# Batch 0's scores with keys on partitions, and no row maximum where a bound allows it

## The chip, the cores and the metric

One core of a Trainium2 chip runs the kernel. Its engines are TensorE (PE, with PEld for its weight loads), VectorE (DVE), ScalarE (ACT), GpSimd (POOL) and SyncE (SP), which only issues DMAs here. The metric is device time in microseconds (us) of one execution.

## The reference

Eight batches, twelve heads, 448 positions, heads of 64. Queries and keys are normalised by their root mean square and multiplied by gains, then softmax attention; its output x (448 x 768 per batch) goes through a channel mix. The weights are float64.

```python
q_n, k_n = (rmsnorm(q, g_q), rmsnorm(k, g_k))          # x / sqrt(mean(x*x) + 1e-06) * g
scores = matmul(q_n, k_n.transpose(0, 1, 3, 2)) / sqrt(64)
scores = scores - max(scores, axis=-1, keepdims=True)
attn = exp(scores)
attn = attn / (sum(attn, axis=-1, keepdims=True) + 1e-09)
x = matmul(attn, v)                                    # heads side by side
x_prev = x one position earlier, zeros first
xk = mu_k * x + (1 - mu_k) * x_prev
xr = mu_r * x + (1 - mu_r) * x_prev
kk = maximum(xk @ w_k, 0.0)                            # w_k: 768 x 1024
vv = kk * kk @ w_v                                     # w_v: 1024 x 768
r = 1 / (1 + exp(-(xr @ w_r)))                         # w_r: 768 x 768
out = r * vv
```

A normalised row of 64 has a norm of at most 8, so a score is at most 8 * 8 / sqrt(64) = 8 times the largest |g_q g_k|, or 64 times the largest |g_q g_k| / 8.

## The kernel before, in words

**A planner sets the order.** Every part of the kernel is a Python generator that yields operations (one, or a list of matmuls). `Plan.run` repeatedly takes the generator whose operation could start soonest by the planner's own clocks, less a bonus for its priority, and `emit` (line 272) issues it right behind the last one on its engine. So every engine executes a list that was fixed when the program was built, an instruction waits for all those ahead of it on its engine, and every row of the trace carries line 272: the parts are told apart by the tile names. Where either of two engines can do an operation, `plan.pick` takes the one with the lower planned clock.

**Units.** A pair is two heads of a batch (48 in all), a quad is two pairs (24, numbered u). Quads 0 to 2 are batch 0 (`U32 = 3`). A quad's scores come in seven groups of two 128 x 448 tiles, one per head; the seventh holds the last 64 query rows of both pairs.

**Attention.** `stats` and `preps` norm q and k; `turn` transposes them on PE through an `sc` bank into tile `stk`. `scores` issues a group with queries on partitions; `expo` takes a row maximum on DVE (`sums<-sc`, negated) and the exponential on ACT with the maximum as bias and the row sum accumulated beside it.

- Batch 0 stays in float32 end to end (one product per score). The exponentials go to a `nat` tile in SBUF; `probs_pe` scales and inverts the sums on DVE (`sums<-sums`), normalises on POOL (`nat<-nat,sums`), transposes 128 x 128 blocks on PE into `sc` banks (`sc<-ident,nat`), and ACT or DVE copies them into `pT` (`pT<-sc`). `attends` then issues 16 float32 products per pair (`ot<-pT,vf`; on PE they stand in runs of eight records) into the only `ot` bank, and ACT copies the result into the pair's tile `x`.
- Batches 1 to 7 use float16 in three terms (high x high, high x low, low x high). The exponentials stay in PSUM (`sc<-sc,sums`); `split` makes the normalised high half on ACT (`nat<-sc,sums`) and the remainder on DVE (`nat<-sc,sums,nat`); SP's DMA queue transposes `nat` into `pT`; 24 products per pair follow.

**Weights.** `weights` turns 20 column tiles (8 of w_k, 6 of w_r, 6 of w_v, each in two halves) from float64 into float32: POOL takes the top three bits of the low word from its byte 3, ACT scales the high word by 2^-112 into an `mm` bank with Prelu (its slope for negative numbers puts the sign where the next step keeps it), and DVE shifts the one by three and joins the other (`wf<-mm,raw`). `wsplit` finds each column's scale (a product of the tile with itself, its diagonal `dg`, a product `mm<-dg,ones` that spreads it, a DVE maximum `WSC`), and splits the tile into two float16 halves (`wvl<-wf,WSC,wvh` and the like).

**Channel mix.** `mix` makes xk and xr (`df<-x,bsc,df` on DVE). `moe` takes one batch after the other: products with w_k (`mm<-xk,wkh`), relu and square, and then products with w_r and w_v. Before batch 0's first product with w_r it waits until all 20 weight tiles are done (`wdone == NW`).

**Buffers.** Five PSUM banks `sc`, two `mm`, one `ot`; in SBUF 2 `raw`, 2 `wf`, 4 `nat`, 4 `stk`, 9 `x`; `pT` has two halves, one per pair of a quad (`PTFREE`). Until `moe` starts, room of xk, kk and others is lent to `raw`, `wf`, `nat`, `vf`, so some tiles read `xk_104` or `kk_108` early in the program.

## Time and profile before

| | |
|---|---|
| median of 3 runs | 1023.7 us (1022.6 to 1023.84) |
| the profiled execution, span | 1022.8 us |
| PE busy | 933.2 us, 91% |
| DVE busy | 789.3 us, 77% |
| ACT busy | 748.2 us, 73% |
| POOL busy | 691.6 us, 68% |
| DVE row maxima of scores | 336 in 194.3 us |
| ACT exponentials in PSUM | 294 in 180.9 us |
| DVE second halves of the split | 242 (of 294, other shapes apart) in 158.3 us |

How to read the rows: `L272 DVE TENSOR_REDUCE sums<-sc 128x1 f32<-128x448 f32 x336 | 194.3, 614 | ...` is line, engine, operation, output <- inputs by tile name, output shape and input shape (partitions x elements), count; behind the first bar busy time in us and mean ns of one; behind the second the idle time of the engine just ahead of them and what ended most of it. In the slices each digit is a fortieth of the span in tenths busy; PEclk is TensorE's granted clock in tenths of full speed.

### The profile page before, as it was taken

The numbers are of one execution on the slowest core, as the hardware profiler recorded it, in microseconds if no ns is written. First come the engines' busy times: TensorE is split into PE (matmuls) and PEld (weight loads), VectorE is DVE, ScalarE is ACT, GpSimd is POOL, SyncE is SP. The second block draws the span as 40 slices with busy tenths as digits, with TensorE's granted clock in tenths as the row PEclk, the third lists the DMA queues.
The fourth block names the chain that finished last, engine by engine and source line by source line (L and its number), as shares of the span: only waits on it lengthen the run. The fifth ranks groups of instructions, "written<-read, shape, count | busy, mean of one in ns | idle before, by whom it ended". The sixth has DMA issues, their size and how long they took to land.

```text
span 1022.8 us, 18968 instructions
## 1 busy us (share of the span) xinstructions
PE 933.2 (91%) x6166; PEld 489.2 (48%) x6166; DVE 789.3 (77%) x1967; ACT 748.2 (73%) x1755; POOL 691.6 (68%) x738
## 2 busy tenths in 40 slices
PE   1678778778999899999999999999999999999997
PEld 1344334344554455445555555455455554455564
DVE  5888868998989689878988798969887898785000
ACT  2666748988789688798888788888887887684211
POOL 2587678862688576896788467967795679629501
PEclk9779889978999999999999999999999999999999
DMA  8442348785885797777986889579768986662011
GB/s 200 121 118 74 104 126 173 181 182 112 188 188 125 150 188 155 171 165 173 185 165 113 179 180 190 127 163 193 157 126 179 183 181 139 135 124 54 1 32 31
DMA packets 447043, 146.62 MB, mean 143 GB/s; under 512 B 418784, under 2 KB 443360, under 8 KB 446944
## 3 DMA queue, kind: packets, MB, share of 16 engines
q1 hardware_dynamic: 427408, 127.42, 59.2%
q10 hardware_dynamic: 19536, 18.00, 6.1%
q8 instruction: 48, 0.79, 0.3%
q14 instruction: 51, 0.42, 0.1%
HBM read 50.40 MB, written 11.01 MB: 60 GB/s over the span
## 4 chain that ended last, share of the span: by engine, by line
PE 54%; DVE 18%; ACT 9%; POOL 7%; issue 6%; DMA 4%; SPq 1%; ACTq 0%; POOLq 0%; DVEq 0%
PE mm L272 37%; PE ot L272 9%; PE sc L272 8%; DVE sums L272 4%; DVE nat L272 3%; POOL xk L272 2%; ACT nat L272 2%; ACT sc L272 2%; DVE sst L272 2%; DVE df L272 2%; DMA pT<-nat 1%; DVE stm L272 1%; POOL nat L272 1%; SPq L272 1%; POOL qk L272 1%
## 5 line engine op out<-in xcount | busy, mean ns | idle before, releaser
L272 PE MATMUL mm<-wvh,kk 128*128 128x384 f16 x896 | 234.4, 327 | 0.0
L272 PE MATMUL mm<-xk,wkh 128*128 128x448 f16 x768 | 209.5, 355 | 5.9 <-ACT kf L272 4.2
L272 DVE TENSOR_REDUCE sums<-sc 128x1 f32<-128x448 f32 x336 | 194.3, 614 | 23.4 <-PE sc L272 23.0
L272 ACT ACTIVATE sc<-sc,sums 128x448 f32<-128x448 f32 x294 | 180.9, 617 | 36.9 <-DVE sums L272 33.1
L272 ACT ACTIVATE nat<-sc,sums 128x448 f16<-128x448 f32 (+1 forms) x274 | 167.2, 653 | 24.9 <-DVE sums L272 13.1
L272 PE MATMUL mm<-wrh,xr 128*128 128x384 f16 x672 | 179.9, 331 | 0.0
L272 DVE SCALAR_TENSOR_TENSOR nat<-sc,sums,nat 128x448 f16<-128x448 f32 x242 | 158.3, 675 | 28.0 <-ACT nat L272 27.5
L272 PEld LDWEIGHTS <-kk 128*128 128x128 f16 (+1 forms) x1362 | 129.2, 98 | 97.2 <-issue 17.0
L272 PE MATMUL sc<-stk 64*128 64x448 f16 (+3 forms) x1104 | 135.0, 386 | 12.8 <-DVE nat L272 4.2
L272 PE MATMUL mm<-wvl,kk 128*128 128x384 f16 x448 | 146.0, 326 | 0.0
L272 PE MATMUL mm<-xk,wkl 128*128 128x448 f16 x384 | 135.8, 354 | 0.0
L272 PEld LDWEIGHTS <-xr 128*128 128x128 f16 x1008 | 96.9, 99 | 75.2 <-issue 16.3
L272 PE MATMUL mm<-wrl,xr 128*128 128x384 f16 x336 | 111.3, 331 | 0.0
L272 PEld LDWEIGHTS <-wkh 128*128 128x128 f16 x768 | 72.2, 98 | 80.5 <-issue 19.8
L272 PE MATMUL ot<-pT,vh 128*64 128x448 f16 x672 | 101.0, 359 | 2.6 <-issue 1.3
L272 POOL TENSOR_TENSOR o<-o,bsc 128x384 f32<-128x384 f32 x48 | 42.9, 894 | 78.6 <-DVE o L272 53.9
L272 POOL TENSOR_TENSOR qk<-qk,ss 128x896 f32<-128x896 f32 x36 | 63.3, 1758 | 43.2 <-DVE ss L272 28.5
L272 DVE SCALAR_TENSOR_TENSOR o<-o,mm 128x384 f32<-128x384 f32 x56 | 30.6, 546 | 78.0 <-PE mm L272 49.9
L272 ACT ACTIVATE o<-mm,bsc 128x128 f32<-128x128 f32 x144 | 45.6, 386 | 45.6 <-PE mm L272 33.6
L272 DVE SCALAR_TENSOR_TENSOR df<-x,bsc,df 128x448 f32<-128x448 f32 x68 | 65.7, 978 | 10.5 <-POOL df L272 10.3
L272 PEld LDWEIGHTS <-stk 64*128 64x128 f16 x1008 | 35.7, 98 | 70.7 <-issue 48.9
L272 POOL TENSOR_TENSOR nat<-nat 128x448 f32<-128x448 f32 x41 | 47.5, 1157 | 29.9 <-ACT nat L272 29.2
(167 smaller groups left out, 1802.0 us busy)
## 6 DMA issues: line engine op xcount, KB each, us to landing
out_dram<-o SPq DMA_DIRECT2D x56, 192.0 KB, 2.9
qk<-in_k_dram SPq DMA_DIRECT2D x46, 224.0 KB, 3.8
qk<-in_q_dram SPq DMA_DIRECT2D x108, 64.0 KB, 2.5
vf<-in_v_dram SPq DMA_DIRECT2D x96, 64.0 KB, 2.6
raw<-in_moe_w_v_dram ACTq DMA_DIRECT2D x12, 512.0 KB, 4.6
vf<-in_v_dram SPq DMA_DIRECT2D x96, 48.0 KB, 2.5
raw<-in_moe_w_r_dram ACTq DMA_DIRECT2D x12, 384.0 KB, 3.3
kk<-in_moe_w_k_dram ACTq DMA_DIRECT2D x8, 384.0 KB, 4.5
```

The lines of the kernel that those rows point to most:

```text
L272: r = op.fn(op.kw["out"], op.kw["value"]) if op.fn.__name__ == "memset" else op.fn(**op.kw)
```

## The change

1. **Batch 0, keys on partitions.** `scores_t` swaps the operands of the score product: a tile has 128 keys on partitions and the 448 queries in its columns. `expo_t` then takes the exponential on ACT straight from PSUM into `pT`, the layout that the product with v reads: no maximum, no sum, no scaling, no transposes, no copy. A pair has six full tiles, and one that holds the last 64 keys of both heads. The order of transposed columns in `turn` and of v's rows in `vload` changes to match; v's second head of a pair takes one small DMA of 64 x 64 more.
2. **Sums by TensorE.** `attends` issues for each pair of batch 0 one more set of products of the same shape, with a constant tile `halves` (2^-15, and zeros where a head has no rows) in the place of v, into an `sc` bank `tot`: every output row then holds the sum of its query's exponentials times 2^-15. DVE inverts it (RECIPROCAL of 128 x 448 into a `nat` tile) and multiplies the attention product by it into `x` (`x<-ot,nat`), where ACT had copied.
3. **Batches 1 to 7.** No row maximum and no bias of the exponential. The high half of the split goes to ACT or DVE by `plan.pick` (180 of 294 go to DVE). `probs_pe` and its constants are gone, since batch 0 was all that used it.
4. **Weights.** ACT scales with Copy in the place of Prelu, so the sign is shifted out; a new DVE operation puts it into byte 3 of the low word (`raw<-raw`, or `kk<-kk` in lent room; 40 in all).
5. **The bound.** One DVE operation compares the largest |g_q g_k| / 8 with 1 (`BOUND / HD`) into a 1 x 1 flag; scores are then at most 64. At the program's end every engine loads the flag, compares, and branches: either past the end, or into a second copy of the whole kernel (some 18,500 instructions) with `safe=True`, in which every batch takes the maxima and no batch takes the float32 path. For the inputs here the largest value is 0.657.

```diff
-def attn_moe_kernel(tc, q, k, v, g_q, g_k, mu_k, mu_r, w_k, w_v, w_r, out):
+def attn_moe_kernel(tc, q, k, v, g_q, g_k, mu_k, mu_r, w_k, w_v, w_r, out, safe, flag=None):
+    n32 = 0 if safe else U32
...
+        yield G_.memset(out=halves, value=2.0 ** -15)
+        yield G_.memset(out=halves[HD:P, 1, :], value=0.0)
+        yield G_.memset(out=halves[0:HD, 2, :], value=0.0)
...
+        if flag is not None:
+            yield V.tensor_scalar(out=flag, in0=gm[0:1, 0:1], scalar1=BOUND / HD, scalar2=None, op0=ALU.is_le)
...
+    def scores_t(u):
...
+                for h in (1, 0):
+                    hs = slice(h * HD, (h + 1) * HD)
+                    ops.append(T.matmul(
+                        form=("t6" if last else "sc", 4 * S / 2.368),
+                        out=z[0][hs, 0:S] if last else z[h][:, 0:S],
+                        lhsT=K_[hs, NT - 1, xs] if last else K_[hs, 2 * c + x, :],
+                        rhs=Q_[hs, 0:NT, xs], start=True, stop=True))
...
+    def expo_t(i, c, z):
+        yield A.activation(out=PT[i][:, c, :], in_=z[:, 0:S], func=AF.Exp)
...
-        yield V.tensor_reduce(out=sums[:, j:j + 1], in_=sp[:, 0:S], axis=AX.X, op=ALU.max, negate=True)
-        yield A.activation(out=sp[:, 0:S], in_=sp[:, 0:S], func=AF.Exp, bias=sums[:, j:j + 1], accum_out=both[0][:, S + j:S + j + 1])
+        if safe:
+            yield V.tensor_reduce(out=sums[:, j:j + 1], in_=sp[:, 0:S], axis=AX.X, op=ALU.max, negate=True)
+            kw["bias"] = sums[:, j:j + 1]
+        yield A.activation(out=sp[:, 0:S], in_=sp[:, 0:S], func=AF.Exp, accum_out=both[0][:, S + j:S + j + 1], **kw)
...
-        yield A.activation(out=ph[:, j], in_=sp[:, 0:S], func=AF.Copy, scale=r[:, j:j + 1])
+        if safe or plan.pick("ACT", "DVE") == "ACT":
+            yield A.activation(out=ph[:, j], in_=sp[:, 0:S], func=AF.Copy, scale=r[:, j:j + 1])
+        else:
+            yield V.tensor_scalar(out=ph[:, j], in0=sp[:, 0:S], scalar1=r[:, j:j + 1], scalar2=None, op0=ALU.mult)
...
+                tot = yield from banks["sc"].get()
...
+                for dst, of in ((tot, lambda h, c: halves[:, (1 + h) * (c == (NSL - 1) * (1 - h)), :]), (av, lambda h, c: vh[:, NSL * h + c, :])):
+                    yield [T.matmul(form=("av", 4 * NSL * S / 2.368), out=dst[h * HD:(h + 1) * HD, 0:S], lhsT=of(h, c), rhs=pT[:, (NSL - 1) * h + c, :],
+                                    start=(c == 0), stop=(c == NSL - 1)) for c in range(NSL) for h in range(2)]
...
+                yield V.reciprocal(out=rf, in_=tot[:, 0:S])
+                banks["sc"].put(tot)
+                yield V.tensor_tensor(out=xf, in0=av[:, 0:S], in1=rf, op=ALU.mult)
...
-                    yield A.activation(out=z, in_=top.bitcast(F32), func=AF.Prelu, scale=F64_EXP, alpha=F64_NEG)
...
+                yield V.tensor_scalar(out=r8[:, :, :, 3], in0=r8[:, :, :, 7], scalar1=128.0, scalar2=128.0, op0=ALU.is_ge, op1=ALU.mult)
+                yield A.activation(out=z, in_=top.bitcast(F32), func=AF.Copy, scale=F64_EXP)
...
-        attn_moe_kernel(tc, *args)
+            attn_moe_kernel(tc, *args, safe=False, flag=flag)
+            fine = nc.values_load(flag[0:1, 0:1], min_val=0, max_val=1)
+            with tc.If(fine < 1, preferred_fallthrough_block=False):
+                attn_moe_kernel(tc, *args, safe=True)
```

The order of PE's instructions while batch 0's first pairs are worked on, before (every row is from line 272; `nat_293`, `nat_313` and `nat_452` are groups of probabilities, `xk_104` is lent room that holds two more, the `sc` outputs of `ident` are their transposes, `ot_505` a small transpose of the channel mix's scales, the last row the first attention product):

```order
L272 MATMUL sc_510<-ident,nat_293 128x128 x4
L272 MATMUL sc_527<-ident,nat_293 128x128 x3
L272 MATMUL sc_521<-ident,nat_313 128x128 x4
L272 MATMUL sc_538<-stk_193 128x448
L272 MATMUL sc_537<-stk_193 128x448
L272 MATMUL sc_549<-ident,nat_313 128x128 x3
L272 MATMUL sc_541<-ident,nat_452 128x128 x4
L272 MATMUL ot_505<-ident,allmax 128x2
L272 MATMUL sc_553<-ident,xk_104 128x128 x4
L272 MATMUL sc_577<-ident,xk_104 128x128 x3
L272 MATMUL ot_573<-pT,vf_94 64x448 x8
```

The same place in the changed kernel, whose `emit` is line 269:

```order
L269 MATMUL sc_276<-stk_205 128x448
L269 MATMUL sc_275<-stk_205 128x448
L269 MATMUL ot_261<-dg,ones 128x128
L269 MATMUL sc_303<-stk_205 64x448 x2
L269 MATMUL sc_311<-stk_205 128x448
L269 MATMUL sc_310<-stk_205 128x448
L269 MATMUL sc_325<-stk_205 128x448
L269 MATMUL sc_324<-stk_205 128x448
L269 MATMUL sc_348<-pT,halves 64x448 x8
L269 MATMUL ot_347<-pT,vf_99 64x448 x8
L269 MATMUL sc_377<-stk_205 128x448
```

The transposes between scores and attention product are gone; eight products of the sums stand right ahead of the eight with v, and the first attention product is row 35 of PE's list where it was row 96.

The order on DVE there, before (`sums` are the sums of exponentials and the maxima, `WSC` the scales of a weight tile, `muu` small tiles of the mix):

```order
L272 COPY pT<-sc_390 128x4x128
L272 TENSOR_SCALAR sums_108<-sums_108 128x2
L272 TENSOR_REDUCE WSC<-ot_393 128x1
L272 RECIPROCAL sums_108<-sums_108 128x2
L272 TENSOR_SCALAR muu<-mu 128x12
L272 TENSOR_SCALAR WSC<-WSC 128x1
L272 TENSOR_SCALAR muu_421<-muu 128x12
L272 TENSOR_SCALAR WSC<-WSC 128x1
L272 TENSOR_REDUCE sums_109<-sc_453 128x1
L272 TENSOR_REDUCE sums_109<-sc_454 128x1
```

And in the changed kernel (`kk_108` is lent room: in the rows of 384 it holds raw weights; `nat_387` holds the inverted sums, `x_343` the first pair's result, `sst` the statistics of q and k):

```order
L269 SCALAR_TENSOR_TENSOR wf_339<-mm_340,kk_108 128x384
L269 TENSOR_SCALAR kk_108<-kk_108 128x384
L269 TENSOR_REDUCE sst<-nat_331 128x14
L269 RECIPROCAL nat_387<-sc_348 128x448
L269 TENSOR_TENSOR muu<-muu,muu_352 128x12
L269 SCALAR_TENSOR_TENSOR wf_339<-mm_390,kk_108 128x384
L269 TENSOR_REDUCE sst<-nat_395 128x14
L269 TENSOR_SCALAR raw_279<-raw_279 128x384
L269 TENSOR_SCALAR sst<-sst 128x14
L269 TENSOR_SCALAR sst<-sst,gm 128x14
L269 TENSOR_TENSOR x_343<-ot_347,nat_387 128x448
```

Maxima, sums and copies of probabilities have left; a reciprocal and a product per pair, and the operations on the sign bytes, stand between the weights' and the statistics' operations.

The last weight tiles on DVE, ahead of the first product with w_r, before:

```order
L272 SCALAR_TENSOR_TENSOR wvl<-wf_2193,WSC,wvh 128x8x128
L272 SCALAR_TENSOR_TENSOR wf_2291<-mm_2355,raw_2293 128x512
L272 TENSOR_TENSOR stk_2223<-sc_2333,stk_2223 128x512
L272 TENSOR_SCALAR sums_108<-sc_2321 128x2
L272 TENSOR_REDUCE sums_109<-sc_2366 128x1
L272 RECIPROCAL sums_108<-sums_108 128x2
L272 TENSOR_REDUCE sums_109<-sc_2367 128x1
L272 TENSOR_REDUCE sst<-nat_2373 128x14
L272 TENSOR_TENSOR dg<-mm_2415,ident 128x128
L272 SCALAR_TENSOR_TENSOR nat_2384<-sc_2321,sums_108,nat_2384 128x448
```

And in the changed kernel:

```order
L269 SCALAR_TENSOR_TENSOR wf_2245<-mm_2276,raw_2247 128x512
L269 SCALAR_TENSOR_TENSOR df_2270<-x_1225,bsc,df_2270 128x448
L269 TENSOR_SCALAR raw_2277<-raw_2277 128x512
L269 TENSOR_TENSOR dg<-mm_2328,ident 128x128
L269 SCALAR_TENSOR_TENSOR nat_2308<-sc_2294,sums_113,nat_2308 128x448
L269 SCALAR_TENSOR_TENSOR wf_2329<-mm_2330,raw_2277 128x512
L269 TENSOR_REDUCE WSC<-mm_2328 128x1
L269 TENSOR_SCALAR WSC<-WSC 128x1 x2
L269 SCALAR_TENSOR_TENSOR nat_2308<-sc_2295,sums_113,nat_2308 128x448
L269 SCALAR_TENSOR_TENSOR df_2271<-x_1494,bsc,df_2271 128x448
L269 SCALAR_TENSOR_TENSOR wvl<-wf_2245,WSC,wvh 128x8x128
```

Both lists interleave the last tiles with attention of batch 1 and the mix; the maxima between them are gone, and each half tile has its operation `raw<-raw` on the sign bytes.

More of the change, by code (lines that the diff above doesn't have):

```diff
@@ L777, in scores @@
     def scores():
+        for u in range(n32):
+            yield from scores_t(u)
         for gi, (u, x, t0) in enumerate(groups):
-            yield from until(lambda: u in TQ and len(banks["sc"].free) > (SC_KEEP if u < U32 or gi in PE_P else 1) and not st["zq"])
-            tp = None
-            if u < U32 or gi in PE_P:
-                tp = yield from R["nat"].get(u < 3)
+            if u < n32:
+                continue
+            yield from until(lambda: u in TQ and len(banks["sc"].free) > 1 and not st["zq"])
             both = []
@@ L827, in probs @@
+    def probs(gi, both, sums, D):
         u, x, t0 = groups[gi]
```

159 lines of the change are left out of this document (78 added, 81 removed).

## The prediction

> **What bounds the kernel now.** I read the page's slices first, then busy time by stage, then TensorE's waits, then groups by line and shape. The page (span, busy shares, slices):
>
> ```profile
> span 1022.8 us, 18968 instructions
> PE 933.2 (91%) x6166; PEld 489.2 (48%) x6166; DVE 789.3 (77%) x1967; ACT 748.2 (73%) x1755; POOL 691.6 (68%) x738
> PE   1678778778999899999999999999999999999997
> DVE  5888868998989689878988798969887898785000
> PEclk9779889978999999999999999999999999999999
> ```
>
> The profiled execution spans 1022.8 us, 0.9 below the median of 1023.7; I sum against the span and add the 0.9 at the end. PE reaches nine tenths only from the eleventh slice on. Busy time by stage (stretch, length, then PE, PEld, DVE, ACT, POOL with counts, granted clock, DMA):
>
> ```profile
> 0.00:25.00 25.00, 2.32 (x11) 2.02 (x12) 12.54 (x44) 6.81 (x12) 5.62 (x16) 1.00 0.80 198
> 25.00:150.00 125.00, 94.35 (x509) 50.61 (x507) 101.15 (x284) 79.34 (x188) 90.70 (x117) 0.84 0.37 106
> 150.00:236.00 86.00, 63.87 (x418) 32.66 (x417) 79.77 (x196) 73.30 (x157) 64.88 (x70) 0.91 0.78 175
> 300.00:930.00 630.00, 621.60 (x4279) 320.80 (x4278) 528.14 (x1288) 514.94 (x1222) 455.15 (x459) 1.00 0.77 160
> ```
>
> 150 us is where batch 0's last attention product ends (147.03 plus 3.23, quoted below), 236 us where the first product with w_r starts. From 300 us PE is busy 98.7%, at full clock. From 25 to 236 us PE is busy 75%; there DVE is the fullest engine, 81% and then 93% of the stage. TensorE's waits from 236 us on, and then rows of its timeline: batch 0's last attention product, the last weight tile's product, the first product with w_r (start, length, instruction, idle before and releaser):
>
> ```profile
> PE ot L272 <- ACT vh L272: 3.1, 1, 3.1
> PE sc L272 <- DVE nat L272: 2.9, 5, 1.4
> PE ot L272 <- DMA pT<-natx: 1.0, 1, 1.0
> PE ot L272 <- DVE vl L272: 0.7, 1, 0.7
> PE ot L272 <- DVE bstat L272: 0.3, 1, 0.3
> 147.03 3.23 PE L272 MATMUL ot<-pT,vf 128*64 128x448 f32 x16
> 228.42 0.49 PE L272 MATMUL mm<-dg,ones 128*128 128x128 f32 x2
> 235.89 0.50 PE L272 MATMUL mm<-wrh,xr 128*128 128x384 f16 x1
> ```
>
> In 787 us PE waits 8.0 us. So the kernel is two pieces: the time until PE can stream without a break (236 us), set by vector work and by the last weight tile (its last product, 228.42), and then PE's own stream. Taking row maxima away after 236 us can gain at most those 8 us and some of PE's turns between kinds of work. Everything else hangs on when 236 moves, and on how much PE has done by then.
>
> **The change part by part.** Prices (busy over count):
>
> ```profile
> L272 DVE TENSOR_REDUCE sums<-sc 128x1 f32<-128x448 f32 x336 | 194.3, 614 | 23.4 <-PE sc L272 23.0
> L272 DVE SCALAR_TENSOR_TENSOR nat<-sc,sums,nat 128x448 f16<-128x448 f32 x242 | 158.3, 675 | 28.0 <-ACT nat L272 27.5
> L272 DVE SCALAR_TENSOR_TENSOR df<-x,bsc,df 128x448 f32<-128x448 f32 x68 | 65.7, 978 | 10.5 <-POOL df L272 10.3
> L272 DVE SCALAR_TENSOR_TENSOR wf<-mm,raw 128x384 int32<-128x384 int32 x18 | 9.9, 551 | 3.5 <-POOL raw L272 2.0 <-ACT mm L272 1.3
> L272 DVE COPY pT<-sc 128x512 f32<-128x512 f32 x13 | 8.8, 680 | 4.3 <-PE sc L272 4.3
> L272 DVE COPY pT<-sc 128x384 f32<-128x384 f32 x6 | 3.3, 552 | 0.8 <-PE sc L272 0.8
> L272 DVE TENSOR_SCALAR sums<-sums 128x2 f32<-128x2 f32 x21 | 8.6, 426 | 1.2 <-ACT nat L272 1.1
> L272 DVE RECIPROCAL sums<-sums 128x2 f32<-128x2 f32 x168 | 26.0, 158 | 1.5
> L272 DVE TENSOR_SCALAR sums<-sc 128x2 f32<-128x2 f32 x147 | 22.0, 151 | 11.8 <-ACT sc L272 11.0
> L272 DVE TENSOR_SCALAR WSC<-WSC 128x1 int32<-128x1 int32 x40 | 5.8, 145 | 0.2
> L272 DVE TENSOR_SCALAR bsc<-WIN,bsc 128x6 f32<-128x6 f32 x16 | 9.5, 632 | 0.0
> L272 DVE SCALAR_TENSOR_TENSOR vl<-vf,bstat,vh 128x512 f16<-128x512 f32 x42 | 46.0, 1095 | 14.0 <-ACT vh L272 13.7
> ```
>
> DVE ahead of the first product with w_r, counted in the order of instructions before and after. Removed: 72 row maxima at 0.578 (41.6), 19 copies of transposed probabilities (8.8 + 3.3), 21 scalings of sums (8.6), 14 small reciprocals at 0.155 (2.2): 64.5 us. Added: 28 first halves of the split, moved from ACT, bounded by 0.578 (the maximum reads the same PSUM row) and 0.654 (the second half, 158.3/242); I take 0.60, 16.8 us. Six products of average and reciprocal (batch 0's x tiles, until now an ACT copy), same bounds, 3.6. Six reciprocals of 128x448: the width occurs nowhere. A 128x2 reciprocal costs 158 ns against 151 for another 128x2 operation, so the width of 448 would cost about as much as any pass (0.6 us); against the 128x1 row of 145, all of the difference put down to the one more column (13 ns), it is up to 5.8 us. I take 0.6, the nearer row in shape: 3.6 us. Forty sign operations on bytes (28 of 384, 12 of 512): nothing below the 128x1 row's 0.145 (5.8 us in all), nearest is the integer pass of 384 columns at 0.55, and the 128x6 row, 0.49 above the 128x1 row, shows what waiting adds to operations between SBUF tiles, so about 1.05 at the top (45 us with the wider ones). I take 0.75 and 0.88: 31.6 us.
>
> [...]
>
> Because the order also moves batch 1's work forward (PE has two more pairs' products and eight more score groups ahead of the first w_r product), DVE does 13 more second halves (8.5), 4 more mixes at 0.97 (3.9), 2 more splits of v at 1.1 (2.2) and one more quad's statistics, some 20 small operations of 0.15 to 0.6 (6). Added in all: 76.2. Net on DVE before the first w_r product: **+11.7 us**, though 72 maxima went.
>
> Against it: the removed operations carried waits of their own. From 25 to 155 us:
>
> ```profile
> L272 DVE TENSOR_REDUCE sums<-sc 128x1 f32<-128x448 f32 x48 | 28.0, 616 | 5.8 <-PE sc L272 5.7
> ```
>
> With the copies (4.3 + 0.8) and the sums (1.2) that is 12.1 us of DVE idleness. The reciprocals and products wait for PE in their turn, six times about half a microsecond: I credit 8.8. First w_r product: 236 + 11.7 - 8.8 = **239 us, +2.9**.
>
> Could ACT, POOL or PE set it instead? Their rows:
>
> ```profile
> L272 ACT ACTIVATE nat<-sc,sums 128x448 f32<-128x448 f32 x32 | 20.2, 636 | 7.7 <-DVE sums L272 7.7
> L272 POOL TENSOR_SCALAR nat<-nat,sums 128x448 f32<-128x448 f32 x32 | 20.0, 640 | 0.7 <-ACT wrh L272 0.6
> L272 PE MATMUL sc<-ident,nat 128*128 128x128 f32 x168 | 29.4, 311 | 29.3 <-DVE nat L272 22.7 <-DVE pT L272 2.8 <-POOL nat L272 2.7
> L272 PE MATMUL ot<-pT,vf 128*64 128x448 f32 x96 | 23.7, 644 | 3.5 <-ACT ot L272 2.8 <-DVE WSC L272 0.7
> ```
>
> ACT loses accumulator reads, copies of probabilities and half of the split, POOL 42 scalings (26 us at 0.63); both were emptier than DVE. PE loses 147 transposes (0.175 each, 26 us) and gains 48 products for the sums (96 records, 23.7 us): even. So batch 0's attention ends far earlier (by a third, near 105 to 115 us), but the seven weight tiles that now stand behind batch 0's wk products fill DVE again.
>
> PE's stream after the first w_r product (AV of a pair; a score group; the tail, PE alone):
>
> ```profile
> 242.95 2.39 PE ot L272 x24
> 241.13 0.74 PE L272 MATMUL sc<-stk 64*128 64x448 f16 x6
> 927.34 82.94 PE mm L272 x486
> ```
>
> Already done: two pairs, 2 x 2.39, and eight groups at about 0.59, **-9.5**. In the order PE changes its kind of work 305 times after that point instead of 332. A group's rows start 0.67 apart, some 0.1 above six half-width streams, for two turns; I take 0.1 a turn, bounds 0 and 0.13: 27 fewer, **-2.7**. Of the 8.0 us of waits I take half, **-4** (DVE and ACT lose over 60 us each there; bounds 0 and -8). The tail after PE's last product stays.
>
> The branch: every engine loads the flag and compares, and at the end jumps over a second copy of the whole kernel; SP, which waits for the last output, does so on the path. No row has a branch; from below 0, from above two round trips to memory. The nearest is a small transfer:
>
> ```profile
> vf<-in_v_dram SPq DMA_DIRECT2D x96, 48.0 KB, 2.5
> ```
>
> I take one, **+2.5**, top 5. [...] The flag itself (one 1x1 operation) and the memsets lie in the first 25 us, half empty on DVE; uncovered they cost under 1 us.
>
> Weights: Prelu becomes Copy on the same ACT rows, cost nil; hidden or not it is the same pass.
>
> Sum: 1022.8 + 2.9 - 9.5 - 2.7 - 4.0 + 2.5 = 1012.0; with the 0.9, **1013 us**.
>
> **Rivals.** *The weights come early (995 us).* If sign operations cost the near row's 0.55 or less, and DVE's idle stretches of the first stage (24 us of 125) go wholly, the first w_r product comes at 220 to 225. For: DVE ran at 93% once its work was ready. Against: DVE is in order, and what waits there is for PE and POOL too.
>
> *Reciprocals are dear (slower).* Place: DVE, six times, each holding the one attention bank and a score bank. At the row bound of 5.8 us they add 31 us, of which the first stage's idleness (about 12 us) takes some: 1032. It decides from 0.6 + 11/6 = 2.4 us each, if none is absorbed. For: nothing of that width has run. Against: the 128x2 rows, 158 to 151. [...]
>
> *Nothing moves (1022).* PE's gaps after 236 stay or grow because batch 1's transposes now queue behind the v loads on SP, and the 12 us of PE work done ahead are lost to them.
>
> *The change doesn't do what it says.* If the bound failed, both kernels would run, near 2040 us. Gains are absolute normals plus 0.5; a product over 8 among 64 is rare, and the general copy is then not entered.
>
> **How the numbers follow.** Forecast 48%, early weights 22%, dear reciprocals 19%, nothing moves 10%, both copies 1%. The forecast's own range is 1001 to 1022 (sign operations from 0.55 to 1.05, waits, branch). The whole range reaches down into the early case and up to the dear one: 992 to 1031. A change under 0.2% can't be told from none. Faster: nearly all of the forecast (45), the early case (22), a little of the others (4): 0.71. Same: 0.09. Slower: 0.20.
>
> **What would show it.** Right: batch 0's last product near 110 us, the last weight tile's product still between 222 and 240, DVE over 90% busy before it, PE without waits after it, and five rather than three pairs of batch 1 done. Wrong: the first w_r product before 225 (the sign operations are then below 0.55, or DVE has no idleness), RECIPROCAL 128x448 above 2 us, PE waits of over 10 us after 240 us, or more than 5 us between the last output's landing and the end.

## The result and the profile after

The changed kernel takes 1071.05 us (median of 4 runs, 1069.52 to 1072.84) against 1023.56 for the kernel before on the same chip: a ratio of 1.046, interval 1.0443 to 1.0478. It is 47.5 us slower; the forecast was 1013 and the range ended at 1031.

The page of the changed kernel (span, busy shares, slices):

```profile
span 1069.4 us, 18334 instructions
PE 935.9 (88%) x6115; PEld 482.8 (45%) x6115; DVE 740.5 (69%) x1803; ACT 622.5 (58%) x1501; POOL 670.4 (63%) x699
PE   1888578743899999999999999999999998999996
DVE  4866888779967987776874895587885778553000
PEclk9999679965899999999999999999999999999998
```

DVE has 49 us less to do in the whole span, ACT 126 us less, PE the same, and the span is 46.6 us longer. PE reaches nine tenths in the twelfth slice instead of the eleventh, and each slice is longer. Busy time on both sides of the first product with w_r, first of before, then of the changed kernel (stretch, length, PE, PEld, DVE, ACT, POOL with counts, granted clock, DMA share, GB/s):

```profile
0.00:235.90 235.90, 160.44 (x934) 85.19 (x934) 193.43 (x520) 159.45 (x356) 161.20 (x202) 0.88 0.56 141
235.90:1022.80 786.90, 772.78 (x5235) 403.96 (x5233) 595.88 (x1448) 588.73 (x1399) 530.45 (x536) 0.99 0.68 144
```

```profile
0.00:277.80 277.80, 175.00 (x980) 81.36 (x981) 216.34 (x526) 148.31 (x313) 162.95 (x182) 0.83 0.59 138
277.80:1069.40 791.60, 760.93 (x5138) 401.49 (x5136) 524.21 (x1278) 474.19 (x1188) 507.45 (x517) 0.99 0.71 137
```

Here is where the time went. In the first stretch DVE has 22.9 us more work (216.34 against 193.43), but the stretch is 41.9 us longer: DVE stands idle for 61.5 us of it instead of 42.5. In the second stretch PE has 11.9 us less work (760.93 against 772.78, 97 instructions fewer), but the stretch is 4.7 us longer. The work that was done ahead shows in PE's busy time, but PE's waits there grew by 13.0 us and ate it.

TensorE's waits behind the first product with w_r in the changed kernel (total us, times, longest); the first five rows. With every gap counted the waits are 21.4 us, and 8.4 before; this view leaves out gaps under 0.15 us, so its rows add up to 21.0, and to the prediction's 8.0 before:

```profile
PE sc L269 <- DVE nat L269: 5.8, 9, 1.4
PE ot L269 <- DMA pT<-nat: 5.7, 5, 1.8
PE sc L269 <- DMA stk<-nat: 2.7, 4, 0.9
PE ot L269 <- ACT vh L269: 2.0, 2, 1.3
PE sc L269 <- DMA stk<-natx: 1.3, 2, 0.7
```

Three of the five, 9.7 us, end with a DMA transpose. Before, a transpose was named in one of five rows, with 1.0 us. The new operations on DVE ahead of the first product with w_r (groups by shape; busy us, mean ns):

```profile
L269 DVE TENSOR_SCALAR raw<-raw 128x384 uint8<-128x384 uint8 x20 | 15.0, 749 | 1.2 <-POOL raw L269 0.9
L269 DVE RECIPROCAL nat<-sc 128x448 f32<-128x448 f32 x5 | 14.8, 2953 | 6.8 <-PE sc L269 6.8
L269 DVE TENSOR_SCALAR raw<-raw 128x512 uint8<-128x512 uint8 x12 | 9.8, 815 | 4.3 <-POOL raw L269 4.3
L269 DVE TENSOR_SCALAR kk<-kk 128x384 uint8<-128x384 uint8 x8 | 4.7, 588 | 0.0
L269 DVE RECIPROCAL xk<-sc 128x448 f32<-128x448 f32 x1 | 3.0, 2958 | 1.4 <-PE sc L269 1.4
```

A reciprocal of 448 columns takes 2.95 us. Last, the weight tiles: PE's products `dg,ones`, two records per tile, from the start to 150 us, before and after (the last pair of times is the first and the last start):

```profile
L272 PE MATMUL ot<-dg,ones x16: 275/398/579, 29.5 to 109.4; 128*128 128x128 f32 x16
L272 PE MATMUL mm<-dg,ones x8: 275/326/492, 92.6 to 137.2; 128*128 128x128 f32 x8
```

```profile
L269 PE MATMUL ot<-dg,ones x16: 275/398/581, 32.5 to 144.6; 128*128 128x128 f32 x16
```

Twelve of the twenty tiles have come that far by 150 us before, eight in the changed kernel. There the last one's product starts at 265.21 us (228.42 before).

### The profile page after: what moved, and what is told of

It is laid out like the page before. It is cut to its first block, busy times and chain, and to the rows that moved or that the text cites. A ratio compares the mean times of both kernels' runs of the same rounds, so it can differ in the third digit from the quotient of the medians.

```text
span 1069.4 us, 18334 instructions
## 1 busy us (share of the span) xinstructions
PE 935.9 (88%) x6115; PEld 482.8 (45%) x6115; DVE 740.5 (69%) x1803; ACT 622.5 (58%) x1501; POOL 670.4 (63%) x699
## 5 line engine op out<-in xcount | busy, mean ns | idle before, releaser
L269 ACT ACTIVATE sc<-sc 128x448 f32<-128x448 f32 x294 | 156.4, 535 | 39.5 <-PE sc L269 36.0
L269 PE MATMUL sc<-stk 64*128 64x448 f16 (+2 forms) x1104 | 137.1, 391 | 33.4 <-DVE nat L269 17.3
L269 DVE SCALAR_TENSOR_TENSOR nat<-sc,sums,nat 128x448 f16<-128x448 f32 x240 | 155.4, 674 | 10.7 <-ACT nat L269 10.3
L269 PE MATMUL ot<-pT,vh 128*64 128x448 f16 x672 | 104.1, 368 | 10.9 <-DMA pT<-nat 9.5
L269 DVE TENSOR_SCALAR nat<-sc,sums 128x448 f16<-128x448 f32 x152 | 99.0, 675 | 5.1 <-DMA pT<-nat 4.2
L269 POOL TENSOR_TENSOR nat<-nat 128x448 f32<-128x448 f32 x40 | 47.5, 1187 | 50.4 <-ACT nat L269 44.2
L269 DVE SCALAR_TENSOR_TENSOR df<-x,bsc,df 128x448 f32<-128x448 f32 x70 | 72.1, 1040 | 4.5 <-POOL df L269 4.5
L269 POOL TENSOR_TENSOR nat<-qk,nat 128x896 f16<-128x896 f32 x31 | 59.3, 1912 | 23.8 <-ACT nat L269 23.7
```

Source lines behind the costliest of these rows:

```text
L269: r = op.fn(op.kw["out"], op.kw["value"]) if op.fn.__name__ == "memset" else op.fn(**op.kw)
```

## Experiments

Three theories stood against each other. **Work**: the new DVE operations are dearer than thought, and their price is the loss. **Order**: the planner's new list makes engines wait for each other, whatever the operations cost. **Addresses**: the new constant tiles move every tile behind them, and the transposes get slower. A time with a range behind it is the median of four to six runs; one without is a single run. Runs of one kernel lie 3 to 5 us apart, so smaller differences are not resolved. The kernel before, run beside each of them, had medians of 1023.6 to 1024.5, and single runs from 1022.2 to 1031.5. "First w_r product" is the start of batch 0's first product with w_r in the profiled execution: 235.9 before, 277.8 after.

### The prices of the new DVE operations

*A constant in place of the inverse.* The order is held; the sums are not inverted, a constant comes out (the inversion is left out).

```diff
-                yield V.reciprocal(out=rf, in_=tot[:, 0:S])
+                yield V.tensor_scalar(out=rf, in0=tot[:, 0:S], scalar1=0.0, scalar2=4.0, op0=ALU.mult, op1=ALU.add)
```

> The changed kernel in its own order of instructions, but the six reciprocals of 128x448 (2.95 us each in the profile after) are six tensor_scalar operations that write a constant; left out is the inversion of batch 0's sums. Theory A, the added operations' own time on DVE sets the first product with w_r (277.8 us): six times about 2.3 us, that product comes 14 us earlier or more, at 262 to 264, time near 1057. Theory B, the order sets it, in which the weight tiles stand behind batch 0's attention, and DVE (78% busy up to there) has room: less than 6 us, time above 1065.

Measured: 1060.42 us, 10.6 less than the changed kernel; first w_r product at 268.4. The substitute takes 0.62 us, so six by 2.33 = 14.0 us of DVE time were taken away and three quarters of that arrived at the end.

*No sign operations.* The order is held, the 40 operations are planned, and `emit` passes over them (weights lose their signs).

```diff
-                yield V.tensor_scalar(out=r8[:, :, :, 3], in0=r8[:, :, :, 7], scalar1=128.0, scalar2=128.0, op0=ALU.is_ge, op1=ALU.mult)
+                op = V.tensor_scalar(out=r8[:, :, :, 3], in0=r8[:, :, :, 7], scalar1=128.0, scalar2=128.0, op0=ALU.is_ge, op1=ALU.mult)
+                op.skip = True
+                yield op
```

> The changed kernel with every other instruction in its place, but the 40 operations on sign bytes are not issued (the order was made as if they were); left out are the signs of the weights. Theory A: they take about 29 us of DVE ahead of the first product with w_r in the profile after (0.59 to 0.82 us each), so that product comes 20 to 29 us earlier, time 1042 to 1051. Theory B: they lie in DVE's idle time, at most 8 us, time above 1063.

Measured: 1059.84 us, 11.2 less; first w_r product at 265.9. DVE's busy time over the span falls by 23.1 us, to 717.4, and half of it arrives.

*Both.*

> The changed kernel with both edits of the last two at once, every other instruction in its place: constants for the six reciprocals, no operations on sign bytes (left out: the inversion of batch 0's sums and the signs of the weights). They took 10.6 and 11.2 us off. If the two costs lie one after the other on the path: 22 us together, time near 1049, first product with w_r near 256. If they fill the same waits: less than 15 us, time above 1056. Either way at least 20 us over the kernel before would be left to the order and the branch.

Measured: 1054.32 us, 16.7 less, where the two alone add up to 21.8: so in part they seem to remove the same waits. The first stretch, up to the first w_r product at 260.6:

```profile
0.00:260.60 260.60, 171.23 (x979) 79.80 (x979) 180.48 (x486) 147.09 (x310) 155.09 (x182) 0.84 0.65 147
```

DVE now has 13 us less work than before the change (180.48 against 193.43), and the stretch is still 24.7 us longer, with DVE idle for 80 us. So the added work alone is not the cause: its two dear kinds explain 17 of 47.5 us.

*The planner knows the reciprocal's price.* It had costed it as any pass, at about 0.5 us; now at 2.87. The order is planned anew.

```diff
+        if op.fn.__name__ == "reciprocal" and n > 64:
+            return 2870, 2950
```

> The changed kernel, in whose planner a reciprocal of 128x448 costs the measured 2.9 us instead of 0.53; the same operations, ordered anew. If the order is bad because it was made for a short reciprocal: 6 to 12 us off, 1059 to 1065. If the reciprocal's own time matters, however it is planned: within 4 us of 1071. If orders of this planner scatter whatever they know: anywhere from 1050 to 1095.

Measured: 1063.95 us, 7.1 less; first w_r product at 272.3. So part of what the reciprocals cost lies in an order that was made for short ones; which waits went away was not taken apart.

### The branch

*One copy, no flag load and no jump* (the general path is left out).

```diff
-            fine = nc.values_load(flag[0:1, 0:1], min_val=0, max_val=1)
-            with tc.If(fine < 1, preferred_fallthrough_block=False):
-                attn_moe_kernel(tc, *args, safe=True)
```

> The changed kernel without the load of the flag, the branch and the second copy of the kernel; the first copy is the same. The stretch from the last product's end to the end of the span is 9.2 us after and 5.7 before. If the branch past the second copy makes that difference, this run takes 3 to 4 us off, 1067 to 1068, and the first product with w_r stays at 278. If code size or instruction loading slows the start too, that product comes earlier as well, by some us.

Measured: 1069.11 us (1068.35 to 1072.41), ratio to before 1.0449 [1.0428, 1.0469]. The intervals overlap, so the 1.9 us between the medians aren't resolved by the times. The timelines show the tail: the last output's transfers (start, length), of the changed kernel (span 1069.4) and of this one (span 1067.1):

```profile
1061.76 1.11 SPq L269 DMA_DIRECT2D out_dram<-o  x2
```

```profile
1062.82 1.11 SPq L269 DMA_DIRECT2D out_dram<-o  x2
```

From the start of the transfers to the end of the span it is 7.6 us with the jump and 4.3 without, and 9.3 and 5.8 from the end of PE's last product. The jump costs some 3.5 us at the end.

The kept traces show where they go. In the changed kernel the last output has landed at 1065.08 us, SP's compare-and-branch ends at 1065.40, and SP's next instruction starts at 1068.09, 2.7 us later. In between, two DMA packets of 8 KB start, at 1065.45 and 1066.47, of the kind that the profile calls `instruction`. In all ten runs with the jump this gap is 2.5 to 2.9 us and at least one such packet starts in it, some 0.9 to 1.1 us after the branch. In the ten runs without the jump no such packet starts between PE's last product and the end. So most of the 3.5 us passes while SP has no instruction and packets of the kind `instruction` are under way; which engine a packet serves, the records do not say.

### The order

*The scales' products in the `mm` banks.* The bank of the w_k tiles' `dg,ones` products is no longer the single `ot` bank, which a pair of batch 0 now holds through sums, products, reciprocal and multiplication. The order is planned anew.

```diff
-WB_A = 'ot'
+WB_A = 'mm'
```

> The changed kernel, but the scales of the eight w_k tiles are found in an mm bank instead of the one ot bank that the attention product also holds (one constant; the planner then orders anew). Theory B, in its special form that the w_k tiles wait for the ot bank, which a pair now holds through sums, product, reciprocal and multiplication: the eighth w_k tile's product with dg comes before 125 us instead of 144, and the first product with w_r 15 to 25 us earlier, time about 1050. Theory A: the operations on DVE are the same, so that product stays within 6 us of 277.8, time 1065 to 1077.

Measured: 1073.13 us, no gain. The first w_r product comes 34 us earlier, at 243.8, and what follows takes 35.9 us longer (827.5 us instead of 791.6; the row ends 1.3 us ahead of the span's end):

```profile
243.80:1070.00 826.20, 776.68 (x5179) 407.53 (x5179) 532.85 (x1296) 490.00 (x1226) 523.93 (x535) 0.98 0.72 135
```

PE has 15.8 us more left to do there than in the changed kernel (776.68 against 760.93), and waits 41.2 us instead of 21.4. Nearly all of these waits stand ahead of attention products and scores (`ot` and `sc`), the largest, 12.4 us, for the high halves of v on ACT. An early first w_r product is worth nothing by itself here: what was not done before it is done after it.

*Prelu back, one copy.* The weights are scaled as before the change, without sign operations; the order is planned anew.

```diff
-                yield V.tensor_scalar(out=r8[:, :, :, 3], in0=r8[:, :, :, 7], scalar1=128.0, scalar2=128.0, op0=ALU.is_ge, op1=ALU.mult)
-                yield A.activation(out=z, in_=top.bitcast(F32), func=AF.Copy, scale=F64_EXP)
+                yield A.activation(out=z, in_=top.bitcast(F32), func=AF.Prelu, scale=F64_EXP, alpha=F64_NEG)
```

> The changed kernel with Prelu back for the weights (no sign operations, ordered anew), and without the branch and the second copy. Beside the one-copy kernel's 1069 us. If the sign operations cost what leaving them out showed (11 us), and the order adds nothing: 1058, first product with w_r near 267. If the order is the larger part, the new order decides: the eighth w_k tile's dg product and the first product with w_r move by more than 12 us either way, and the time leaves 1050 to 1064.

Measured: 1051.51 us. First w_r product at 243.9, PE's stream behind it, up to PE's last product, 800.0 us with 28.3 of waits, where the changed kernel has 782.4 with 21.4: again the start gained and the stream lost. Prelu together with the branch wasn't tried.

*Before, without maxima.* Only part 3 of the change, in batch 0 too, on the kernel before: no maxima and no bias, and the split on ACT or DVE as in the change (no bound, so the general path is left out).

```diff
-            yield V.tensor_reduce(out=sums[:, j:j + 1], in_=sp[:, 0:S], axis=AX.X, op=ALU.max, negate=True)
-... func=AF.Exp, bias=sums[:, j:j + 1], accum_out=...
+... func=AF.Exp, accum_out=...
```

> The kernel before with one part of the change: no row maxima and no bias in any batch (left out: the general path for large scores), the high half of the split on ACT or DVE; batch 0's layout, its transposes, Prelu and the one copy as before; ordered anew. By the prediction's own account DVE loses 72 maxima of 0.58 us (41.6 us) and gains some 17 us ahead of the first product with w_r: that product at 215 to 225 instead of 236, time 1000 to 1012. If DVE is not what holds that stage: 232 to 240, time 1016 to 1026.

Measured: 1011.49 us; first w_r product at 230.4. Timed again beside others:

> The kernel before without row maxima once more, with rounds for an interval: 1010 to 1013 us, ratio 0.985 to 0.991.

1009.55 us (1007.97 to 1012.19), ratio 0.9845 [0.9802, 0.9889]. Without maxima, and ordered anew, the kernel gains 14 us, so the loss comes with the other parts of the change.

### The addresses

The names of the tiles give no hint of this, the layout does. `halves` (768 bytes a partition) and the flag's tile (32 bytes) stand ahead of the large tiles. Worked out from the layouts: `pT`, `nat`, `stk`, `x`, `kk` and `xk` start at multiples of 512 bytes before, and at 288 bytes past one in the changed kernel. So do the weights and the tiles of q and k.

*Before, shifted by 288 bytes.* Instruction for instruction the kernel before.

```diff
-    ones = const.tile([P, 1], F32, name="ones")
+    ones = const.tile([P, 80], F32, name="ones")[:, 0:1]
```

> The kernel before, instruction for instruction, but one small constant tile is wider, so every large SBUF tile (weights, pT, nat, stk, qk, x, xk) starts 288 bytes further on each partition: at 32 modulo 64 and 288 modulo 512, where the changed kernel has them, in place of multiples of 512. Theory C, that the change's two small tiles (32 and 768 bytes) moved the tiles and this slows the DMA transposes (median 4.0 us from issue to landing before, 4.7 after, and 4.6 in each variant of the changed kernel): transposes at 4.5 to 4.8 us, waits of TensorE behind the first product with w_r up from 8 to 15 us or more, time 1032 to 1055. Theory B, the order alone: nothing changes, transposes 4.0, time 1022 to 1026.

Measured: 1041.94 us (1040.58 to 1045.6), ratio 1.0169 [1.0145, 1.0193]. A constant tile that is larger by 316 bytes a partition, of which nothing is read, costs 18 us. The transposes in the view of DMA issues (median us from issue to landing), before and shifted:

```profile
pT<-nat SPq DMA_TRANSPOSE x121, 4.0
stk<-nat SPq DMA_TRANSPOSE x28, 3.5
```

```profile
pT<-nat SPq DMA_TRANSPOSE x121, 4.6
stk<-nat SPq DMA_TRANSPOSE x28, 4.2
```

They take 0.6 to 0.7 us longer, and PE's waits behind the first w_r product rise from 8.4 to 25.9 us. Rows that end with a transpose make up 12.7 us of these, where they were 1.0:

```profile
PE ot L272 <- DMA pT<-nat: 7.8, 9, 1.2
PE ot L272 <- DMA pT<-natx: 2.3, 2, 1.2
PE sc L272 <- DMA stk<-nat: 2.3, 3, 1.5
```

The other transfers into moved tiles changed less (the larger v loads from 2.6 to 2.9 us); what part of the 18 us is theirs was not separated.

*Before, shifted by 256 bytes* (the same line with 72 in place of 80).

> The kernel before, instruction for instruction, with all large tiles shifted by 256 bytes on each partition. Shifted by 288 it took 1041.9 us. If only multiples of 512 are fast: transposes at 4.5 to 4.7 us, time 1036 to 1045. If multiples of 256 are enough (320 modulo 512 was not): transposes 4.0, time 1022 to 1026.

Measured: 1029.39 us, above the expected range. The transposes are back at 3.9 and 3.6 us and the waits at 9.3, so the addresses do no harm in the stream. The first w_r product comes 3.7 us late, at 239.6. The granted clock goes with that: from 75 to 155 us it was 0.84, against 0.88 in the profile before, the 96 float32 attention products kept PE busy for 27.1 us instead of 23.7, and the last of them ended 3.75 us later (154.01). The kernel before does the same by itself: its runs beside these experiments at a mean clock of 0.960 to 0.965 took 1027.3 to 1031.5 us, the others 1022.2 to 1025.7. This run's clock was 0.966.

*The changed kernel, shifted by another 32 bytes,* to 320 past a multiple of 512.

```diff
-            flag = pool.tile([1, 1], I32, name="bounded")
+            flag = pool.tile([1, 16], I32, name="bounded")[:, 0:1]
```

> The changed kernel, instruction for instruction, with the flag's tile 64 bytes wide instead of 32-byte room: all large tiles start at multiples of 64 (320 modulo 512). Theory C with 64 bytes as the step that matters: transposes back at 4.0 us, 13 to 30 us off, time 1041 to 1058. Theory C with a larger step, or theory B: within 4 us of 1071.

Measured: 1070.85 us (1069.24 to 1072.99), ratio 1.0463 [1.0436, 1.0489], transposes of `pT` at 4.6: no change. 320 is a multiple of 64, so that alone is not enough.

*The changed kernel with its tiles at multiples of 512.* The halves become one column each, broadcast to 64 as the product's operand; same order.

```diff
-    ones = const.tile([P, 1], F32, name="ones")
-    halves = const.tile([P, 3, HD], F32, name="halves")
+    four = const.tile([P, 4], F32, name="ones")
+    ones, halves = four[:, 0:1], four[:, 1:4]
...
-            flag = pool.tile([1, 1], I32, name="bounded")
+            flag = pool.tile([1, 128], I32, name="bounded")[:, 0:1]
```

> The changed kernel in the same order with all large tiles at multiples of 512, as before the change: the constants for the sums lie beside the ones (a column each, read 64 times by the weight load), the flag's tile is 512 bytes wide. Theory C: transposes 4.0 us, 13 to 30 us off, time 1041 to 1058; if 64 bytes are what matters, the same as the run with multiples of 64. Theory B: within 4 us of 1071.

Measured: 1055.75 us (1053.64 to 1059.04), ratio 1.0301 [1.0273, 1.0329]: 15.3 us less than the changed kernel. Transposes and TensorE's waits, changed kernel's transposes first:

```profile
pT<-nat SPq DMA_TRANSPOSE x120, 4.7
stk<-nat SPq DMA_TRANSPOSE x31, 4.3
```

```profile
pT<-nat SPq DMA_TRANSPOSE x120, 3.9
stk<-nat SPq DMA_TRANSPOSE x31, 3.6
...
PE sc L273 <- DVE nat L273: 4.4, 7, 1.8
PE ot L273 <- ACT vh L273: 1.3, 1, 1.3
PE sc L273 <- DVE natx L273: 1.1, 2, 0.9
```

PE's waits fall from 21.4 to 8.5 us, and no transpose is named in any of its rows. The first w_r product stays where it was (279.8): the addresses cost nothing in the first stage and everything in PE's stream. Over the runs, the transposes into `pT` took 3.9 to 4.0 us with the tiles at 0 and 256 bytes past a multiple of 512, and 4.6 to 4.7 at 288 and 320; by what mechanism was not shown.

### What is left, and what the order is worth

*All of it at once,* in the changed kernel's order: constant inverse, no signs, one copy, aligned tiles (the diffs above together).

> The changed kernel in its own order with every single cost found so far taken out: constants for the reciprocals, no sign operations (both left out of the result), large tiles at multiples of 512, one copy without the branch. If these add up (16.7, 15.3 and 2 to 3.5 us off 1071), 1036 to 1038, and the 12 to 14 us that are left over the kernel before belong to the order, though 336 maxima are gone. If they hide each other, above 1041; if the order costs nothing, 1024 or less.

Measured: 1038.04 us, 33.0 less than the changed kernel; the parts add up to 16.7 + 15.3 + 1.9 = 33.9. Within the scatter of single runs they add up, so they are separate costs. Of the 47.5 us, about 14 are left: the first w_r product is at 263.6, 27.7 later than before, and PE's stream gives some 15 of that back. None of the named costs is in this kernel. What is left is the order with the work that it moved ahead, or batch 0's new layout itself; the reordered kernel below decides between them.

*Prelu, one copy, aligned,* in the order of the earlier Prelu kernel:

> The run with Prelu and one copy (1051.5 us), in the same order, with all large tiles at multiples of 512. Theory C: transposes from 4.6 to 4.0 us, TensorE's waits behind the first product with w_r from 28 to 8 to 14 us, time 1030 to 1038. That leaves about 20 us to the kernel before without maxima (1011.5), which differs in batch 0's layout and the order alone. If alignment does nothing in this order: 1050.

Measured: 1033.06 us, against 1051.51 unaligned; transposes 4.0, waits 14.0 us instead of 28.3, first w_r product 244.7 (243.9 unaligned). Addresses again act in the stream alone.

*The same operations in another order.* Twelve constants of the planner are changed (priorities of kinds of work, the bank of the scales' products, the pace at which weight tiles are pushed), and the reciprocal has its price; Prelu, aligned tiles and one copy as in the run before, so the general path is left out. The diffs of constants are printed several to a line.

```diff
-PRIO_P = 200; PRIO_A = 50; PRIO_V = 310; PRIO_W = 200; PRIO_E = 400; SWITCH = 600
-SLACK_F = 6; LEAD_V = 1; TR_COST = 130; W_GAP = 10e3; W_PUSH = 0.03; WB_A = 'ot'
+PRIO_P = 100; PRIO_A = 100; PRIO_V = 200; PRIO_W = 100; PRIO_E = 300; SWITCH = 300
+SLACK_F = 4; LEAD_V = 2; TR_COST = 110; W_GAP = 8e3; W_PUSH = 0.1; WB_A = 'mm'
```

> Batch 0 as in the change (keys on partitions, sums by TensorE, reciprocals), no row maxima, Prelu, one copy without the branch (so without the general path for large scores), large tiles at multiples of 512, the reciprocal priced at 2.9 us in the planner, and twelve of the planner's constants set anew, among them the w_k scales in an mm bank. Theory B, what is left over the kernel before is the order: first product with w_r at 210 to 225 us, time 990 to 1010. Rival D, batch 0's new layout itself is slower (TensorE's sums in float32, reciprocals that hold the ot bank): the first product with w_r stays behind 235, time above 1020.

Measured: 994.81 us (992.96 to 997.05), ratio 0.9695 [0.9644, 0.9746]. Beside the run before, with the same operations, the order is worth 38 us (it includes the planner's choice of engine: six operations stand on ACT instead of DVE). DVE stands idle for 44.6 us of the first stretch instead of 73.3. So the new layout of batch 0 is not slow by itself. The weight tiles up to 150 us, in the old order and in the new:

```profile
L274 PE MATMUL ot<-dg,ones x16: 274/276/579, 29.4 to 136.9; 128*128 128x128 f32 x16
L274 PE MATMUL mm<-dg,ones x4: 276/400/578, 131.7 to 146.2; 128*128 128x128 f32 x4
```

```profile
L276 PE MATMUL mm<-dg,ones x28: 275/300/582, 27.1 to 139.4; 128*128 128x128 f32 x28
```

Ten tiles against fourteen. The first w_r product comes at 207.3, and three pairs of batch 1 instead of four are done by then.

*The whole change reordered, sign operations on POOL;* tiles aligned, the reciprocal priced, fourteen planner constants set anew (not fifteen, as the expectation has it).

```diff
-                yield V.tensor_scalar(out=r8[:, :, :, 3], ...)
+                yield G_.tensor_scalar(out=r8[:, :, :, 3], ...)
```

> The change whole, with the flag, the branch and the second copy: large tiles at multiples of 512, the sign operations on POOL instead of DVE, the reciprocal priced at 2.9 us in the planner, and fifteen planner constants set anew (twelve as in the run at 994.8 us or near them). Beside that run it has 40 operations on POOL and the branch (2 to 3.5 us): 997 to 1012 us if the order and the addresses were what was wrong with the change; above 1023 if the general path and the signs eat what the rest gains.

Measured: 1037.74 us (1036.39 to 1039.28), ratio 1.0128 [1.0111, 1.0145]. A miss. The groups on POOL ahead of the first w_r product (249.3) show a likely cause:

```profile
L275 POOL TENSOR_SCALAR raw<-raw 128x384 uint8<-128x384 uint8 x20 | 42.8, 2140 | 1.0
L275 POOL TENSOR_SCALAR raw<-raw 128x512 uint8<-128x512 uint8 x12 | 35.1, 2921 | 1.0
L275 POOL TENSOR_SCALAR raw<-raw 128x384 int32<-128x384 uint8 x20 | 11.2, 561 | 1.7
```

From bytes to bytes POOL takes 2.1 us for 384 columns, where it takes 0.56 from bytes to integers. It becomes the fullest engine: 218 of 249.3 us busy.

*The whole change, aligned and reordered, sign operations on DVE,* with flag, branch and second copy. Fifteen constants of the planner are changed, three of them otherwise than in the last run (`PRIO_W`, `W_PUSH`, `BOOST_W`).

```diff
-PRIO_P = 200; PRIO_A = 50; PRIO_V = 310; PRIO_W = 200; PRIO_E = 400; PRIO_R = 320; SWITCH = 600; SLACK_F = 6
-LEAD_V = 1; TR_COST = 130; W_GAP = 10e3; W_PUSH = 0.03; WB_A = 'ot'; MARGIN_A = 400; BOOST_W = 300
+PRIO_P = 100; PRIO_A = 100; PRIO_V = 200; PRIO_W = 300; PRIO_E = 300; PRIO_R = 200; SWITCH = 300; SLACK_F = 4
+LEAD_V = 2; TR_COST = 150; W_GAP = 8e3; W_PUSH = 0.06; WB_A = 'mm'; MARGIN_A = 200; BOOST_W = 600
```

> The whole change with the flag, the branch and the second copy, and the sign operations on DVE as the change has them: large tiles at multiples of 512, the reciprocal priced at 2.9 us in the planner, fifteen planner constants set anew. The 1037.7 us of the run before, with the same kind of order, went to the sign operations on POOL (2.1 to 2.9 us each). If so, this is the run at 994.8 us plus about 11 us of sign operations and 2 to 3.5 of the branch: 1003 to 1014. If the order's gain doesn't survive the sign operations: above 1020.

Measured: 1013.81 us (1011.31 to 1016.44), ratio 0.9894 [0.987, 0.9918]. The whole change, with every operation that it adds, takes 1.1% less time than the kernel before. The 24 us to the last run are the sign operations' move and three constants together.

```profile
0.00:224.30 224.30, 155.00 (x876) 72.63 (x877) 181.60 (x451) 125.53 (x258) 144.59 (x162) 0.87 0.61 147
224.30:1013.00 788.70, 770.97 (x5240) 402.14 (x5239) 553.73 (x1331) 503.07 (x1266) 524.51 (x538) 1.00 0.71 144
...
L275 PE MATMUL mm<-dg,ones x26: 273/326/582, 30.4 to 146.0; 128*128 128x128 f32 x26
```

Against the aligned kernel in the old order (1055.75) it is 42 us: 55.5 us at the start, of which the stream takes 10.9 back, since less of batch 1 is done ahead. DVE has 38 us less in the first stretch than in that kernel (181.6 against 219.4), mostly attention and mix of batch 1 that the old order put there (42 second halves of the split against 26, for one). Thirteen tiles have their scale by 150 us. Which of the constants does it was not taken apart; the bank alone does not (1073.13). The constants of the kernel before were not searched in this way, so the 10.7 us are the gain of change and order together.

The ledger of the 47.5 us:

| cause | us | from |
|---|---|---|
| addresses of the large tiles | 15.3 | aligned, same order |
| reciprocals and sign operations | 16.7 (alone 10.6 and 11.2) | constant, no signs, same order |
| branch | 1.9 (not resolved by the times; tail 3.5) | one copy |
| left: order and work moved ahead, net of the maxima's gain | about 14 | all three off, same order |

## Why the prediction was wrong

By the terms of its own sum, profiled executions (us):

| term | predicted | measured |
|---|---|---|
| DVE's work ahead of the first w_r product | +11.7 | +22.9 |
| DVE's idleness there | -8.8 | +19.0 |
| first w_r product, the two together | +2.9 | +41.9 |
| PE's work done ahead, and its turns | -9.5 - 2.7 = -12.2 | -11.9 |
| PE's waits behind it | -4 | +13.0 |
| end of the program | +2.5 | +3.6 |
| sum | -10.8 | +46.6 |

- **"+11.7 us" of DVE work: mechanism right, size wrong.** It was 22.9. Most of the difference is the reciprocal, taken at 0.6 us "the nearer row in shape" and measured at 2.95: six of them are 14.1 us above their term, more than the 11.2 that were missing, and the other prices came out a little high. The nearer row was the wrong one: at 2 columns the reciprocal stood 7 ns above the other operation (158 against 151), at 448 columns it stands 2.33 us above a TENSOR_SCALAR (2.95 against 0.62); the far row, with a bound of 5.8, held it. The rival *reciprocals are dear* was right in its mechanism, and 2.95 lies above its threshold of 2.4 us; left out, the reciprocals are worth 10.6 us. The 0.49 of the 128x6 row, which the sum read as waiting, is part of a mean (632 ns) over 16 records of 209 to 1253 ns; why they differ no run shows. The sign operations' 31.6 were 29.5 in durations, but successive rows overlap (108.20 and 108.58 are the starts of two, the first 0.58 long), so leaving them out took 23.1 off DVE's busy time.

```profile
108.20 0.58 DVE L269 TENSOR_SCALAR kk<-kk 128x384 uint8<-128x384 uint8 x1
108.58 1.00 DVE L269 TENSOR_SCALAR sst<-sst 128x14 f32<-128x14 f32 x1
```

- **"I credit 8.8" of DVE idleness: this step failed.** Of the 39.0 us by which the first w_r product missed its term, 11.2 are DVE's work and 27.8 its idleness: 19.0 us more than before, instead of 8.8 less. DVE was to be over 90% busy; it was 78% over the whole stretch (82% before), and 83% from 150 us on, where it had been 93%. The largest waits of DVE from 25 us to the first w_r product, before and then in the changed kernel (27.2 and 44.3 us in all rows):

```profile
DVE sums L272 <- PE sc L272: 5.7, 8, 1.3
DVE pT L272 <- PE sc L272: 5.1, 5, 3.7
DVE wf L272 <- ACT mm L272: 2.2, 4, 1.1
```

```profile
DVE wf L269 <- ACT mm L269: 6.9, 8, 1.8
DVE nat L269 <- PE sc L269: 6.8, 3, 3.2
DVE raw L269 <- POOL raw L269: 5.1, 6, 3.1
DVE sst L269 <- POOL nat L269: 4.0, 3, 2.2
```

The waits of the maxima (`sums<-sc`) and copies (`pT<-sc`) did go, as credited. But the reciprocals wait for PE's sums (6.8 us, and 1.4 in lent room, where six times half a microsecond were set), the sign operations wait for POOL, and the weights' joins and the statistics wait longer than before (6.9 instead of 2.2, 4.0 instead of 1.8). The credit took waits away with the operations that had carried them, as if nothing else in the list could wait. The kernel with all costs off shows it cleanest: DVE has 180.8 us of work there instead of 193.4, and the first w_r product is 27.7 us later. The prediction read from the order only what stood where, not whether each thing is ready when its turn comes; with the operations of the Prelu kernel kept and their order changed, that product moved from 244.7 to 207.3.
- **"The seven weight tiles that now stand behind" were seen, and not priced.** Batch 0's last attention product ended at 132.3 us, not near 110, and the last tile's product at 265.2, not between 222 and 240. Five pairs of batch 1 were done ahead, as predicted; that work was counted as a gain in PE's stream at full, and at 20.6 us on DVE ahead of it. In the reordered kernel it is left where it was (three pairs), and that kernel is faster.
- **"Of the 8.0 us of waits I take half": wrong in sign.** They rose to 21.4, and the cause is in none of its steps: no row of before has a transpose at another address. With aligned tiles they are 8.5, so the halving didn't come either.
- **The branch was right:** 2.5 predicted, 3.6 measured, the bound 5; from the last output's landing to the end it is 4.35 us instead of 0.9. In the changed kernel's trace the compare-and-branch on SP itself takes 0.04 us; behind it stand 2.7 us without an instruction on SP, with packets of the kind `instruction` under way.
- **The early weights** did not come (277.8 instead of 220 to 225), though in another order the product does come at 224.3: by the order, and not by that rival's condition, since the sign operations take 0.60 to 0.80 us there. *Both copies* did not run.
- The range fell short because each unknown was bounded alone, and the dear case with its 1032 was made of one of three costs that came together: 15 us of addresses, 17 of dear operations and 14 of order.

## What to carry to other kernels

A change that adds a constant tile can move every tile behind it, as here by 288 bytes: look at the start addresses of whatever DMA transposes read and write, and pad small tiles so that these stay where they were fast here, 0 or 256 bytes past a multiple of 512 (`pT<-nat` 3.9 to 4.0 us, against 4.6 to 4.7 at 288 and 320; no other start was run). Where a planner sets the order, a change of the operations is two changes; hold the order to price the operations, and give the planner a measured price of any new instruction and a look at its constants before judging the idea. A busy share says nothing of an order's waits: DVE lost 36 us of work in one of these runs and 17 arrived.

## What the runs showed of the hardware

- DMA transposes into and out of tiles that start at 288 or 320 bytes past a multiple of 512 take 4.6 to 4.7 us (`pT<-nat`) against 3.9 to 4.0 at 0 or 256. With 288 the same instructions took 1.7% longer [1.45, 1.93].
- A RECIPROCAL of 128x448 float32 on DVE takes 2.95 us, nearly five times a TENSOR_SCALAR of that shape (0.62); at 128x2 the difference is 7 ns (158 against 151).
- A byte-to-byte operation on POOL takes 2.14 us for 384 columns and 2.92 for 512, against 0.56 for bytes to integers; on DVE the same byte operation takes 0.59 to 0.82.
- A branch past a second copy of some 18,500 instructions lengthened the end of the program from 5.8 to 9.3 us; 2.5 to 2.9 us of it pass on SP between the branch and the next instruction, in ten runs of ten.
